# A fused attention and softplus FFN kernel: single load steps in the bias stage, four relus moved to ScalarE, four score tiles moved into round 0, and one round order for rounds 1 to 13

## The chip, the cores and the metric

The kernel runs on one core of a Trainium2 chip. The metric is the device time of one execution in microseconds (us). Five engines work beside each other, each through its own list of instructions in order: TensorE (PE; its weight loads are PEld), VectorE (DVE), ScalarE (ACT), GpSimd (POOL) and SyncE (SP), which here only issues DMA transfers. ScalarE issues some transfers too.

## What is computed

```python
scores = scale * np.matmul(q, k.transpose(0, 1, 3, 2))       # 4 batches, 8 heads, 576 x 576, head size 64
x = (psi_rel / psi_i)[..., None]                             # from the distance |i - j| and the row i
bias = np.maximum(x @ w1 + b1, 0.0) @ w2                     # a small MLP, 32 hidden units, one bias per head
attn = softmax(scores + bias.transpose(2, 0, 1))             # along the row, with 1e-9 in the divisor
h = (attn @ v, laid out as 2304 x 512) @ w_in                # FFN, 512 -> 2048 -> 512
out = (np.maximum(h, 0.0) + np.log1p(np.exp(-np.abs(h)))) @ w_out
```

The bias depends on head and position alone, so it is made once and kept in DRAM.

## The kernel before, in words

**Bias stage** (L868 to L888). 36 steps `s`, each for 16 rows of the bias. `emit_hid` makes four hidden tiles `m` of a step (relu of `lw` times a row's constant): three on VectorE, the fourth on ScalarE if `s` is in `RELU_ACT`, else on VectorE too. It runs `LEAD` = 5 steps ahead; 23 `m` tiles exist. `emit_mm` multiplies them on TensorE into `acc` (two of them), `emit_rows` copies `acc` on ScalarE in two pieces into a tile `e` (a ring of five, pool `wk`) and SP stores it to `e_d` in DRAM. Bias tiles `b` of 128 rows are loaded back from `e_d` by `emit_bias(pr, t)`, `t` from 0 to 8 (tiles 0 to 3 head one, 5 to 8 head two, tile 4 the last 64 rows of both). Tile 4 needs the last store.

**Rounds.** A round `n` (0 to 15) handles one pair of heads of one batch. Its nine score tiles `t` are made one round ahead: S is the product on TensorE into one of four PSUM places, A on VectorE adds the bias, takes the row's extreme and so empties the place (`first`), X is the exponential on ScalarE (`second`). T turns a block (TensorE), V copies it out of PSUM (suffix a on ScalarE, d on VectorE), P0 to P4 are the products with `vn`. I inverts the row sums, R turns them, C copies them and stores them to `r_d` (ScalarE's queue), G loads them back spread over 64 rows as `rb`, O multiplies the output by `rb` on VectorE, Y stores it. Z, ZA, ZX, ZL are S, A, X, L for the round itself, used in round 0. D is a dummy transpose. v, k, q, w, b issue loads; B are steps on the FFN's weights, whose tokens bring them in beside attention.

Within the bias stage some score tiles are made already: `STAGE` lists them by step, D for a whole tile of round 0 and R for a tile of round 1 that ScalarE copies out of PSUM unchanged (`raw`, L356), so that the bias can be added later.

**What sets the order.** The order of instructions on an engine is the order in which the program issues them: `ROUND0`, `ROUND1`, `ROUND` (rounds 2 to 13), `ROUND14` and so on are lists of tokens, a suffix such as `/2` naming the PSUM place. In rounds 0 and 1 the loads hang on token positions (`LOADS0`, `LOADS`), and O's and C's followers are deferred by a number of tokens (`defer`, `RB_AFTER` = 24). In the bias stage loads follow `LOAD_AT` and `early`. A DMA waits in its issuer's list until what it needs is there, and what stands behind it waits too. SP's list shows a few loads ahead of their place in the code, where nothing held them.

After round 16 comes the FFN on TensorE alone, unchanged here.

## Time and profile before

| | us |
|---|---|
| three runs | 673.45, 675.04, 809.87 |
| median of them | 675.04 |
| the profiled execution | 675.52 |
| its span, first to last instruction | 673.7 |
| TensorE busy | 643.7 (96%) |
| ScalarE busy | 513.0 (76%) |
| VectorE busy | 499.2 (74%) |

The profile is of one execution; times in it count from the span's start. "Busy" leaves out waiting. A row of waits or of the chain names the releaser: the work whose end let the engine go on. L numbers are lines of the kernel before.

### The profile page before, as it was taken

Reading aid. Unit: us, or ns where it says so; the run is one execution under the profiler, and the core shown is the slowest. Engines: PE = TensorE matmul, PEld = TensorE weight load, DVE = VectorE, ACT = ScalarE, POOL = GpSimd, SP = SyncE. Lnnn points to the kernel's source line nnn. Section 1 sums busy time; section 2 is a strip of 40 time slices with the busy share of each in tenths; the row PEclk is TensorE's granted clock in tenths of the full one; section 3 lists DMA queues with packets and bytes.
Section 4 is the critical chain, followed back from the end, with each engine's and each line's share of the span. In section 5 each row is a group of like instructions: output and inputs, shape, how many; then the busy total and the mean of one; then the engine's idle time right before and its main releaser. Section 6 shows DMA issues by size and latency. Waiting matters only on the chain.

```text
span 673.7 us, 13202 instructions
## 1 busy us (share of the span) xinstructions
PE 643.7 (96%) x4807; PEld 479.0 (71%) x4807; DVE 499.2 (74%) x1084; ACT 513.0 (76%) x1059; POOL 32.8 (5%) x103
## 2 busy tenths in 40 slices
PE   5689789999999998999999999999999999999997
PEld 2124446766767665778888888888888888888886
DVE  6976659999998998787786965796774556556564
ACT  6798769999999998897785867785775665665654
POOL 0000101111111110000000000000000000000000
PEclk9879789999999999999999999999999999999999
DMA  5876938868879646551321204230200322202220
GB/s 150 310 239 226 344 118 277 280 226 291 282 242 283 212 150 209 163 191 44 142 78 48 102 9 151 74 121 33 78 17 0 113 76 106 82 0 87 70 95 32
DMA packets 51040, 96.84 MB, mean 144 GB/s; under 512 B 7440, under 2 KB 19104, under 8 KB 50976
## 3 DMA queue, kind: packets, MB, share of 16 engines
q1 hardware_dynamic: 50208, 95.34, 42.1%
q8 instruction: 38, 0.62, 0.4%
q10 hardware_dynamic: 768, 0.66, 0.3%
q14 instruction: 26, 0.21, 0.1%
...
## 4 chain that ended last, share of the span: by engine, by line
PE 88%; DMA 5%; ACT 3%; DVE 1%; SPq 1%; issue 1%; ACTq 0%; DVEq 0%
PE y L842 29%; PE h L784 29%; PE o L470 11%; PE s L347 6%; PE s L411 4%; PE acc L236 3%; PE t L347 3%; DMA e_d<-e 2%; PE t L411 1%; ACT e L257 1%; PE o L347 1%; PE o L411 1%; DMA dist<-in_c_dist_dram 1%; DMA a<-w_d 1%; DMA b<-e_d 1%
## 5 line engine op out<-in xcount | busy, mean ns | idle before, releaser
L784 PE MATMUL h<-x,wi 128*128 128x512 f32 (+1 forms) x960 | 211.7, 370 | 0.1
L842 PE MATMUL y<-wo,g 128*128 128x512 f32 x864 | 209.8, 391 | 0.0
L784 PEld LDWEIGHTS h<-x,wi 128*128 128x128 f32 x960 | 169.5, 189 | 33.2 <-DVE wi L757 0.5
L842 PEld LDWEIGHTS y<-wo,g 128*128 128x128 f32 x864 | 161.3, 188 | 33.6 <-DVE g L816 0.2
L807 DVE SCALAR_TENSOR_TENSOR u<-u,e 128x512 f32<-128x512 f32 (+1 forms) x80 | 51.0, 638 | 103.4 <-ACT l L804 103.1
L383 ACT ACTIVATE p<-p,m 128x576 f32<-128x576 f32 x144 | 110.4, 768 | 5.9 <-DVE m L365 2.4
L800 ACT ACTIVATE e<-h 128x512 f32<-128x512 f32 (+1 forms) x80 | 44.2, 553 | 77.3 <-PE h L784 77.2
L470 PE MATMUL o<-pt,vn 128*64 128x256 f32 (+3 forms) x640 | 83.5, 424 | 0.0
L365 DVE CUSTOM_DVE_ANT_0 p<-s,b 128x576 f32<-128x576 f32 x79 | 58.5, 753 | 10.0 <-ACT e L257 3.3
L814 ACT ACTIVATE g<-l 128x512 fp32r<-128x512 f32 (+1 forms) x80 | 46.8, 585 | 19.3 <-DVE l L811 9.8
L347 PE MATMUL s<-kn,qn 64*128 64x288 f32 (+1 forms) x416 | 59.2, 419 | 0.2 <-ACT p L358 0.2
L470 PEld LDWEIGHTS o<-pt,vn 128*64 128x64 f32 (+1 forms) x640 | 37.6, 138 | 27.8 <-issue 8.7
L816 DVE TENSOR_TENSOR g<-l,g 128x512 fp32r<-128x512 f32 (+1 forms) x80 | 50.4, 629 | 3.7 <-ACT g L814 3.7
L236 PE MATMUL acc<-m,coef 128*32 128x512 f32 (+17 forms) x352 | 38.3, 537 | 15.0 <-ACT e L257 7.7
L316 ACT ACTIVATE pt<-s 128x384 f32<-128x384 f32 (+1 forms) x94 | 44.7, 483 | 8.1 <-ACT r L524 4.6
L811 DVE TENSOR_TENSOR l<-l,u 128x512 f32<-128x512 f32 (+1 forms) x80 | 50.6, 632 | 0.0
L809 DVE SCALAR_TENSOR_TENSOR l<-h,l 128x512 f32<-128x512 f32 (+1 forms) x80 | 50.5, 631 | 0.0
L804 ACT ACTIVATE l<-u 128x512 f32<-128x512 f32 (+1 forms) x80 | 47.2, 589 | 2.9
L801 ACT ACTIVATE e<-e 128x512 f32<-128x512 f32 (+1 forms) x80 | 47.2, 590 | 2.5
L803 ACT ACTIVATE u<-e 128x512 f32<-128x512 f32 (+1 forms) x80 | 47.2, 590 | 2.6
L223 DVE TENSOR_SCALAR m<-lw,pb 128x576 f32<-128x576 f32 (+17 forms) x122 | 44.3, 443 | 1.0 <-PE acc L236 1.0
L411 PEld LDWEIGHTS s<-ident,p 64*128 64x128 f32 x672 | 32.4, 141 | 17.3 <-DVE m L365 7.4
...
## 6 DMA issues: line engine op xcount, KB each, us to landing
e_d<-e SPq DMA_DIRECT2D x36, 295.5 KB, 3.4
...
```

What stands on the lines that cost most here:

```text
L236: nc.tensor.matmul(acc[32 * g:32 * g + 32, lo:hi], lhsT=coef.rearrange("p o h -> p (o h)"), rhs=hid[s, g][:, lo:hi], start=True, stop=True ...
L347: nc.tensor.matmul(ps[at:at + w, half, :SH], lhsT=q_n[n][rows, hd, c0:c0 + w], rhs=k_n[n][rows, hd], start=True, stop=True, tile_position= ...
L365: nc.vector.tensor_tensor_reduce(prob[n, t].rearrange("p (a c) -> p a c", a=2), st_["ps"], bias[pr, t].rearrange("p (a c) -> p a c", a=2), ...
L383: nc.scalar.activation(p, p, AF.Exp, bias=st_["m"], scale=-1.0, accum_out=ssum[n][:, PLACE.index(t):PLACE.index(t) + 1],)
L411: nc.tensor.transpose(ps[:, a, i], src[rows], ident[rows, 64 * a:64 * a + 64], tile_position=(64 * a, 0))
L470: nc.tensor.matmul(o[up, half, 0:w], lhsT=v_n[n][rows, jb, hd], rhs=pt[n, jb][rows, c0:c0 + w], start=(jb == 0), stop=(jb == 4), tile_posi ...
L784: nc.tensor.matmul(ps[:, :nb], lhsT=wi[f][:, a, 128 * c:128 * c + 128], rhs=xs[bi, c][:, x_, :nb], start=(i == 0), stop=(i == 11),)
L807: nc.vector.scalar_tensor_tensor(u, u, -1.0, e, op0=ALU.add, op1=ALU.subtract)
L809: nc.vector.scalar_tensor_tensor(l, ps, 0.0, l, op0=ALU.max, op1=ALU.add)
L811: nc.vector.tensor_tensor(l, l, u, op=ALU.subtract)
L816: nc.vector.tensor_tensor(g[:, 1], l, g[:, 0], op=ALU.subtract)
L842: nc.tensor.matmul(y, lhsT=g[:, a, 128 * ts:128 * ts + 128], rhs=wo[f][:, w_], start=(first and i == 0), stop=(last and i == 2),)
```

## The change

Line numbers in rows of the changed kernel are smaller, by 12 in the stage and by up to 48 at the end.

- Constants: `dist`, `tab`, then `wts`; the first batch's k and q no longer stand ahead of the stage.
- `RELU_ACT` gains steps 3, 6, 9 and 12.
- k and q of batches 0 and 1 are loaded singly after steps 0, 2, 5, 8; bias tiles 0, 5, 1, 6, 2, 7, 3, 8 singly after steps 11 to 35, where they came in pairs. k of batch 2 comes ahead of bias tile 4, q behind `vn`.
- Raw tiles of round 1: R11, R13, R18 and R14 go; tiles 1, 3, 8 and 4 are made in round 0 (S1, S3, S8, S4).
- `ROUND0` is rewritten with its loads as tokens and without D; round 1 uses `ROUND`. `defer`, `LOADS`, `LOADS0`, `ROUND1`, `STEADY` go. All `rb` loads are issued by SP.

```diff
-LOADS = {22: "b", 4: "q", 0: "v", 34: "w", 6: "k", 25: "b", 23: "b", 10: "b", 31: "b"}
-LOADS0 = {17: "k", 28: "v1", 71: "w", 6: "q", 59: "v"}
-RELU_ACT = {s for s in range(30) if s % 3 or not s} | {32}
-
-LOAD_AT = (2,)
-LATE = 3
+RELU_ACT = {s for s in range(30) if s % 3 or s < 13} | {32}
+
+LOAD_AT = {0: (0, "k"), 2: (0, "q"), 5: (1, "k"), 8: (1, "q")}
+EARLY = ((11, 0), (14, 5), (18, 1), (22, 6), (26, 2), (29, 7), (34, 3), (35, 8))
 STAGE = """
-21:D00 21:R15 24:R16 25:R10 26:R12 26:D01 27:D05 29:R17 31:R11 31:R13 32:D02 33:D06 33:R18
-34:R14
+21:D00 21:R15 24:R16 25:R10 26:R12 26:D01 27:D05 29:R17 31:D02 33:D06
 """
...
-    nc.sync.dma_start(out=wts, in_=mlp)
     nc.sync.dma_start(out=dist, in_=c_dist.to_broadcast([128, S]))
     nc.sync.dma_start(out=tab[:, 0:212], in_=c_tab)
+    nc.sync.dma_start(out=wts, in_=mlp)
...
-                queue(n).dma_start(
+                nc.sync.dma_start(
                     out=t[64 * hd:64 * hd + 64, lo:hi],
...
-    emit_load(0)
     nc.sync.dma_start(out=ident, in_=c_id)
...
-    early = {8 * t + 7: (t, t + 5) for t in range(3)}
+    early = {s: (t,) for s, t in EARLY}
...
         if s in LOAD_AT:
-            emit_load(1 + LOAD_AT.index(s))
-        for t in early.pop(s - LATE, ()):
+            emit_load(*LOAD_AT[s])
+        for t in early.pop(s, ()):
             emit_bias(0, t)
...
-    for t in (3, 8, 4):
-        emit_bias(0, t)
+    emit_load(2, "k")
+    emit_bias(0, 4)
     emit_load_v(0)
-    emit_load(2)
+    emit_load(2, "q")
...
         if n < 3:
-            tiles = [(1, t) for t in ((), range(5), range(5, 9))[n]]
+            tiles = [(1, t) for t in ((0,), (1, 2, 4, 3), (8, 7, 5, 6))[n]]
...
-        toks = {0: ROUND0, 1: ROUND1, N - 2: ROUND14, N - 1: ROUND15, N: ROUND16}.get(n, ROUND).split()
+        toks = {0: ROUND0, N - 2: ROUND14, N - 1: ROUND15, N: ROUND16}.get(n, ROUND).split()
...
-            if tok == "C" and n not in STEADY:
-                defer(RB_AFTER, lambda n=n: units["r", n][2]())
```

`ROUND0` after the change:

```
v1 Z7/0 T10/o S1/1 ZA7 V10/a Z3/2 T20/0 ZX7 A1 V20/a k q T00/o S3/1 ZA3 X1 V00/d Z8/0 T30/2 ZX3 A3
V30/a ZL1 ZL2 A2 S8/1 ZA8 X3 T40/2 V40/a A0 ZX8 Z4/0 A8 ZL3 T12/o V12/d X2 T22/2 V22/a S4/1 w ZA4
T02/o V02/d X0 L0 T32/2 V32/a A4 ZX4 ZL4 I T01/2 V01/d R/0 T11/o C G v V11/a T21/2 V21/d A7 X8 P0 X4
L4 A5 P1 T31/0 V31/a T41/2 V41/d X7 A6 P2 X5 b L1 L2 X6 L3
```

What moves on the engines, at three places.

SP in the bias stage, before; `e_d<-e` is a step's store, kn and qn are k and q of a batch, `b<-e_d` a bias tile:

```order
L869 DMA ident<-in_c_id_dram 128x128
L261 DMA e_d<-e 128x591 x3
L279 DMA kn<-in_k_dram 128x2x288
L285 DMA qn<-in_q_dram 128x1152
L261 DMA e_d<-e 128x591 x8
L306 DMA b<-e_d 128x576
L308 DMA b<-e_d 128x576
L261 DMA e_d<-e 128x591 x8
L306 DMA b<-e_d 128x576
L308 DMA b<-e_d 128x576
L261 DMA e_d<-e 128x591 x8
```

The same place after:

```order
L837 DMA ident<-in_c_id_dram 128x128
L249 DMA e_d<-e 128x591
L267 DMA kn<-in_k_dram 128x2x288
L249 DMA e_d<-e 128x591 x2
L273 DMA qn<-in_q_dram 128x1152
L249 DMA e_d<-e 128x591 x3
L267 DMA kn<-in_k_dram 128x2x288
L249 DMA e_d<-e 128x591 x3
L273 DMA qn<-in_q_dram 128x1152
L249 DMA e_d<-e 128x591 x3
L294 DMA b<-e_d 128x576
L249 DMA e_d<-e 128x591 x3
```

The pair k and q behind the third store, and the pairs of bias tiles, are taken apart; k and q of the first batch join them among the stores.

ScalarE at the end of the bias stage, before; `e<-acc` are a step's two copies, `p<-s` a raw copy, `p,ss<-p,m` an exponential, `pt<-` a V copy:

```order
L358 ACTIVATE p<-s_82 128x576
L257 ACTIVATE e<-acc,tab 128x64
L257 ACTIVATE e<-acc,tab 128x527
L358 ACTIVATE p<-s_83 128x576
L257 ACTIVATE e<-acc,tab 128x48
L257 ACTIVATE e<-acc,tab 128x543
L257 ACTIVATE e<-acc,tab 128x32
L257 ACTIVATE e<-acc,tab 128x559
L358 ACTIVATE p<-s_82 128x576
L257 ACTIVATE e<-acc,tab 128x16
L257 ACTIVATE e<-acc,tab 128x575
L383 ACTIVATE p,ss_117<-p,m 128x576
```

The same place after:

```order
L371 ACTIVATE p,ss_117<-p,m 128x576
L245 ACTIVATE e<-acc,tab 128x64
L245 ACTIVATE e<-acc,tab 128x527
L245 ACTIVATE e<-acc,tab 128x48
L245 ACTIVATE e<-acc,tab 128x543
L245 ACTIVATE e<-acc,tab 128x32
L245 ACTIVATE e<-acc,tab 128x559
L245 ACTIVATE e<-acc,tab 128x16
L245 ACTIVATE e<-acc,tab 128x575
L371 ACTIVATE p,ss_117<-p,m 128x576 x2
L304 ACTIVATE pt<-o 128x2x3x64
L371 ACTIVATE p,ss_117<-p,m 128x576
```

The raw copies between the steps' copies are gone (R11, R13 and R18 here), and behind the last copy ScalarE goes to two exponentials and the first V copy of round 0.

ScalarE in rounds 0 and 1, before, around the row sums of round 0; `r<-t` is C's copy, `r_d<-r` its store, `rb<-r_d` the loads of G, `p,ss<-p,m` exponentials, `pt<-` V copies:

```order
L524 ACTIVATE r<-t 9x128
L525 DMA r_d<-r 9x128
L383 ACTIVATE p,ss_118<-p,m 128x576
L383 ACTIVATE p_1099,ss_119<-p_1099,m 128x576
L316 ACTIVATE pt<-s_82 128x2x3x64 x2
L531 DMA rb<-r_d 64x576
L531 DMA rb<-r_d 64x320
L531 DMA rb<-r_d 64x256
L524 ACTIVATE r<-s_83 9x128
L525 DMA r_d<-r 9x128
```

SP from the loads behind bias tile 4 on, after:

```order
L280 DMA vn<-in_v_dram 128x640
L273 DMA qn<-in_q_dram 128x1152
L280 DMA vn<-in_v_dram 128x640
L267 DMA kn<-in_k_dram 128x2x288
L273 DMA qn<-in_q_dram 128x1152
L667 DMA r<-in_moe_w_in_dram 128x512
L516 DMA rb<-r_d 64x576
L516 DMA rb<-r_d 64x320
L516 DMA rb<-r_d 64x256
L280 DMA vn<-in_v_dram 128x640
L294 DMA b<-e_d 128x576
```

The three loads of `rb` left ScalarE's list, where an exponential of round 0, one of round 1's and two copies stood ahead of them, and stand on SP, ahead of a load of `vn` and a bias tile; ScalarE keeps the copy and the store.

## Rows read from the trace of the kernel before

**Rows 1.** The page's head: span and number of instructions.

```profile
span 673.7 us, 13202 instructions
```

**Rows 2.** Chain of waits: start us, length us, engine, tile, line, count.

```profile
118.14 0.54 PE o L347 x4
...
130.48 0.54 PE o L347 x4
```

**Rows 3.** Busy us by stretch (count of instructions), granted clock, DMA share, GB/s.

```profile
62.80:80.60 17.80, 12.66 (x135) 7.65 (x131) 10.99 (x31) 14.55 (x38) 2.57 (x9) 0.81 0.83 304
80.60:99.30 18.70, 15.44 (x166) 8.54 (x164) 10.86 (x28) 10.57 (x26) 1.80 (x5) 0.91 0.55 181
```

In rows 3 and 8 the columns are length, then busy time of PE, PEld, DVE, ACT and POOL.

**Rows 4.** The same, sum over 10.2 to 62.8 us.

```profile
sum 52.60, PE 44.52 PEld 13.07 DVE 45.82 ACT 46.11 POOL 0.00; mean PE 11.13 PEld 3.27 DVE 11.46 ACT 11.53 POOL 0.00
```

**Rows 5.** Timeline of ScalarE, bias stage: start, length, work, [idle before <- releaser].

```profile
10.20 0.90 ACT L257 ACTIVATE e<-acc,tab 128x576 f32<-128x576 f32 x2 [0.91 <-PE acc L236]
11.00 0.71 ACT L221 ACTIVATE m<-lw,pb 128x496 f32<-128x496 f32 x1
11.60 1.72 ACT L257 ACTIVATE e<-acc,tab 128x560 f32<-128x560 f32 x4
...
21.43 0.90 ACT L257 ACTIVATE e<-acc,tab 128x448 f32<-128x448 f32 x2 [1.91 <-DMA e_d<-e]
...
33.70 0.90 ACT L257 ACTIVATE e<-acc,tab 128x304 f32<-128x304 f32 x2 [1.06 <-DMA e_d<-e]
```

**Rows 6.** Chain of waits from the start to round 1.

```profile
1.17 4.58 DMA dist<-in_c_dist_dram
...
14.80 6.53 DMA e_d<-e
...
62.80 3.81 DMA e_d<-e
...
67.30 4.25 DMA b<-e_d
...
75.23 2.12 PE o L470 x8
...
79.56 1.12 PE o L470 x8
...
85.85 3.74 DMA rb<-r_d
```

**Rows 7.** Timeline of SP's queue, bias stage.

```profile
14.21 0.49 SPq L285 DMA_DIRECT2D qn<-in_q_dram  x1
```

**Rows 8.** Busy us in stretches of two us, as in rows 3.

```profile
20.00:22.00 2.00, 0.57 (x8) 0.00 (x0) 2.00 (x7) 0.56 (x2) 0.00 (x0) 1.00 1.04 398
...
24.00:26.00 2.00, 2.00 (x16) 0.26 (x8) 2.00 (x8) 1.46 (x5) 0.00 (x0) 0.50 0.55 213
```

**Rows 9.** Timeline of TensorE around the end of the bias stage.

```profile
64.12 0.40 PE L411 MATMUL s<-ident,p 64*128 64x64 f32 x6 [1.04 <-ACT p L358]
...
71.87 0.58 PE L411 MATMUL t<-ident,p 64*128 64x64 f32 x6 [3.12 <-ACT p L383]
```

**Rows 10.** Timeline of VectorE, round 1: the multiplication by rb.

```profile
89.72 0.82 DVE L490 TENSOR_TENSOR x<-o,rb 128x256 f32<-128x256 f32 x2 [4.15 <-DMA rb<-r_d]
```

**Rows 11.** Groups by line, 0 to 66 us: count, busy us, mean ns, idle before.

```profile
L223 DVE TENSOR_SCALAR m<-lw,pb 128x576 f32<-128x576 f32 (+17 forms) x122 | 44.3, 443 | 1.0 <-PE acc L236 1.0
...
L221 ACT ACTIVATE m<-lw,pb 128x464 f32<-128x464 f32 (+17 forms) x22 | 14.2, 658 | 4.6 <-DVE pb L200 4.6
...
L358 ACT ACTIVATE p<-s 128x576 f32<-128x576 f32 x9 | 5.9, 666 | 0.6 <-PE s L347 0.6
```

**Rows 12.** The page's DMA issues: count, KB each, median us to landing.

```profile
e_d<-e SPq DMA_DIRECT2D x36, 295.5 KB, 3.4
```

**Rows 13.** Timeline of ScalarE's queue, rounds 0 and 1.

```profile
79.89 0.55 ACTq L525 DMA_DIRECT2D r_d<-r  x1
...
84.67 1.79 ACTq L531 DMA_DIRECT2D rb<-r_d  x3
```

More of the change, by code (lines that the diff above doesn't have):

```diff
@@ L50 @@
 """
-STEADY = range(2, 17)
 SETS = ((2, 4), (3, 8), (7, 5, 6), (1, 0))
 ROUND0 = """
-A6 A2 Z7 T10/1 A7 Z3 T20/0 V20/a T30/o A0 T00/2 ZA7 V00/d V30/a V10/a A1 A5 D6 Z8 X7 X2 ZX7 ZA3 X5
-X6 ZA8 A3 ZX3 ZX8 Z4 ZA4 ZL1 ZL3 ZX4 A8 D14 T22/2 T40/1 T32/o ZL4 V32/d T02/0 V22/a V02/a T01/o X0
-T11/2 V40/d T21/1 V11/a ZL2 V01/d V21/d L2 T12/0 P0 X8 L0 X1 I V12/d T41/1 A4 P1 X4 T31/0 R/2
-V41/a C P2 V31/d L3 X3 L4 L1
-"""
-ROUND1 = """
-I S4 T20/0 S3 A4 T11/1 A3 T00/2 S2 P3 X4 V00/d V20/a T02/0 V11/d T12/2 V02/a R/1 C P4 T41/0 S7
-T22/1 S0 A2 O V12/a T01/o V41/a T10/0 V22/d L4 B0 T21/2 V01/a X3 A7 S1 V10/d P0 V21/a A0 T31/0
-X2 T32/2 S5 X7 A1 P1 S6 V31/a V32/d X0 S8 B1 T30/1 X1 B2 L0 A5 T40/0 V30/a B3 L1 A8 V40/a X8 A6
-X6 L3 P2 B4 X5 L2
+v1 Z7/0 T10/o S1/1 ZA7 V10/a Z3/2 T20/0 ZX7 A1 V20/a k q T00/o S3/1 ZA3 X1 V00/d Z8/0 T30/2 ZX3 A3
+V30/a ZL1 ZL2 A2 S8/1 ZA8 X3 T40/2 V40/a A0 ZX8 Z4/0 A8 ZL3 T12/o V12/d X2 T22/2 V22/a S4/1 w ZA4
+T02/o V02/d X0 L0 T32/2 V32/a A4 ZX4 ZL4 I T01/2 V01/d R/0 T11/o C G v V11/a T21/2 V21/d A7 X8 P0 X4
+L4 A5 P1 T31/0 V31/a T41/2 V41/d X7 A6 P2 X5 b L1 L2 X6 L3
 """
@@ L509, in inv @@
         nc.vector.reciprocal(s_, s_)
-    def queue(n):
-        return nc.scalar if n < 2 else nc.sync
     def u_r(n):
@@ L593, in emit @@
         elif kind in ("Z", "ZA", "ZX"):
-            stage(("s", n, *a), u_s, ("Z", "ZA", "ZX").index(kind))
+            stage(("s", n, *a), u_s, ("Z", "ZA", "ZX").index(kind), *on)
         elif kind == "L":
@@ L610, in emit @@
                 stage(("x", n - 1), u_x, 0)
-                if n not in STEADY:
-                    defer(8, lambda: stage(("x", n - 1), u_x, 1))
         elif kind == "B":
@@ L616, in emit @@
                 stage(("b", i), u_bits, *a)
-                if a[0] == 4 and n not in STEADY:
-                    defer(8, lambda: stage(("b", n - 1), u_bits, 5))
         elif kind in ("k", "q"):
-            emit_load(n + 3, kind)
+            emit_load(n + (a[0] if a else 3), kind)
         elif kind == "v":
-            emit_load_v(n + 2)
+            emit_load_v(n + (a[0] if a else 2))
         elif kind == "w":
@@ L650, in emit @@
             assert False, tok
-    waiting = []
-    def defer(k, f):
-        waiting.append([k, f])
-    def passed():
-        for w in list(waiting):
-            w[0] -= 1
-            if w[0] < 0:
-                waiting.remove(w)
-                w[1]()
     def bits(pl, src, eng, pb_=None):
@@ L975, in tile_log_bias_attention__then__softplus_ffn @@
             s_use[0] = 0
-        toks = {0: ROUND0, 1: ROUND1, N - 2: ROUND14, N - 1: ROUND15, N: ROUND16}.get(n, ROUND).split()
-        for i, tok in enumerate(toks):
-            load = {0: LOADS0, 1: LOADS}.get(n, LOADS if n > N - 2 else {}).get(i)
-            if load in ("k", "q"):
-                emit_load(n + 3, load)
-            elif load == "v":
-                emit_load_v(n + 2)
-            elif load == "v1":
-                emit_load_v(n + 1)
-            elif load == "w":
-                pre_load(n)
-            elif load == "b" and tiles:
-                emit_bias(*tiles.pop(0))
-            emit(n, tok)
-            if tok == "C" and n not in STEADY:
-                defer(RB_AFTER, lambda n=n: units["r", n][2]())
-            passed()
-    while waiting:
-        passed()
+        toks = {0: ROUND0, N - 2: ROUND14, N - 1: ROUND15, N: ROUND16}.get(n, ROUND).split()
+        for tok in toks:
+            emit(n, tok)
     es_m.close()
```

1 line of the change is left out of this document (removed).

## The prediction

> **What bounds the kernel now.** The profiled execution took 675.5 us, of which the span is 673.7 [rows 1]; the median of the three runs is 675.0, so the sum below is made on 675.5 and reads the same on the median. A difference under 2% (13.5 us) is about what a measurement of this kernel cannot tell from no change.
>
> I read the chain of waits first, then busy time by stage. From about 106 us on, the chain is TensorE work only: round 3 and round 4 repeat the same score tile 12.34 us apart [rows 2]. The change leaves everything from round 2 on in its old order, so only the time before round 2, which starts at 99.3 us, can move. That time has three stretches: the bias stage to 62.8, round 0 of 17.8 and round 1 of 18.7 us [rows 3]. A round costs 12.34 when TensorE is full, so round 1 alone carries 6.4 us of waste.
>
> In the bias stage the engine with least room is ScalarE: from the first bias row's copy to the last it works 46.11 of 52.60 us [rows 4]. VectorE runs ahead of it. Of the 6.5 us idle, 1.91 and 1.06 are waits for a store `e_d<-e` to land [rows 5]: the five `e` tiles are a ring, and step 8 needs step 3's store, which the chain shows taking 6.53 us [rows 6]; step 17 needs step 12's. The first was issued at 14.80, right behind the pair k and q of batch 1 (288 and 576 KB; q's issue is at 14.21 [rows 7]), the second in the wake of the first two bias loads. TensorE was busy 0.57 us of 20 to 22, and in 24 to 26 its granted clock is 0.50 (1.2 instead of 2.4 GHz) [rows 8]; after a gap of 3.12 us before 71.87 [rows 9] a P block (a product with v) takes 2.12 us at 75.23 where one at 79.56 takes 1.12 [rows 6]; after one of 1.04 us before 64.12 nothing of the kind shows.
>
> Behind the stage the chain goes: last store 3.81 us, bias tile 4's load 4.25, then the slow P block, then the load `rb<-r_d`, for which VectorE sits idle 4.15 us [rows 6, 10].
>
> **The change, part by part.**
>
> *Constants' order.* `dist` is issued first instead of second. Its issue stood at 1.17 [rows 6], so it may start 0.43 earlier; k and q no longer follow it at once. `wts`, also needed, now goes third. Bounds: 0.4 us lost (if `wts` lands last) to 1.2 gained. I take 0.6, since the large k and q stop sharing the engines with it: first copy at 9.6 instead of 10.2.
>
> *Four relus to ScalarE.* A relu of 496 columns occupies it from 11.00 to 11.60 [rows 5], so steps 3, 6, 9, 12 (528, 480, 432, 384 columns) cost 0.63, 0.59, 0.54, 0.50. Step 3's fits in the 0.91 us in which ScalarE waits for the first accumulator [rows 5]; the others add 1.6 us to the engine that bounds. VectorE saves four at 0.44 [rows 11] and gains nothing, for it was ahead. This part alone is a loss.
> The Trainium skill, "ScalarE: Activation LUTs", section "Rules for kernel authors", says to put relu on VectorE, not ScalarE, and budgets about 0.3 us plus 0.83 ns an element; an estimate by that page is 0.7, 0.66 and 0.62, so 2.0 us, and the sum would be 0.4 longer than with the row's occupancy. The trace agrees in direction: 658 ns on ScalarE against 443 on VectorE.
>
> *Four raw copies fewer.* R11, R13 and R18 stood before the last copy, R14 behind it. One takes 0.67 [rows 11], about 0.1 of it overlapped as for the relu: 1.6 us off ScalarE before the end. This cancels the relus, so ScalarE's floor stays 46.1.
>
> *Loads in small steps.* k and q of batches 0 and 1 now stand singly after steps 0, 2, 5, 8; one k and seven bias tiles come singly later. The ring allows a store five steps of about 1.2 us, less copy and issue: some 4.7, against a median landing of 3.4 [rows 12]. At 400 GB/s, about what the engines reach in 20 to 22 [rows 8], a 288 KB load adds 0.7 and q's 576 KB adds 1.4: inside for the former, at the edge for the latter. So I let both waits go (3.0 us). With them goes what caused the half-clock stretch in rows 8, in which ScalarE waits for accumulators too, so I take 1.1 of the remaining 3.5 us of small pieces. Idle 2.4: last copy ends at 9.6 + 46.1 + 2.4 = 58.1, against 62.8, so 4.7 us gained. Bounds: idle 0 (55.7) and unchanged 6.5 (62.2).
>
> *Round 0.* The four score tiles go to TensorE in round 0 (4 x 0.54 [rows 2], beside 12.66 busy of 17.8 [rows 3], much of that at half clock), and VectorE reads them straight from PSUM. ScalarE has the same 13 exponentials either way, one transposed copy more and R14 less, so it keeps its 14.5 us [rows 3], hidden under the rest as long as it is fed. What sets the end is bias tile 4: store 3.81 plus load 4.25 and two issues, 8.9 us after the last copy as now. Bias tiles 3 and 8 are issued later (after steps 34 and 35); they are wanted ahead of tile 4, and the work before them (two or three tiles on VectorE) covers them. From tile 4's landing (71.55) to round 1's first score tile (80.6) it takes 9.1 now, with the same work behind the tile in the new order: subtraction, exponential, reciprocal, transposes, three P blocks. At full clock the first P block is 1.0 shorter, and the transposes and the second block around it I put at 0.8: 7.3 us. TensorE runs out of other work about 2 us before tile 4's transpose (eight score tiles and nine transposes are some 6 to 7 us, ahead of a point some 10 us after the last copy, with ScalarE's pace spread between), between the gap that kept the clock and the one that lost it [rows 9]; the dummy transposes are gone too. So 16.2 to 18.0; I take 16.9. Round 1 starts at 58.1 + 16.9 = 75.0, against 80.6.
>
> *Round 1* takes the steady order. `rb` now is issued by SP right behind its store instead of 24 tokens later on ScalarE's queue: today the row sum's store goes at 79.89 and the load not before 84.67 [rows 13]. About 9 us (its 4.5 KB store 2.5, an estimate under the 295 KB stores' 3.4, three issues 1.8 [rows 13], load 3.74 [rows 6], handovers) after its transpose it is there; in the new order x wants it about 9 us after that transpose. So the 4.15 us wait shrinks to at most one. SP's queue waits there for the store; behind it stand v, a bias tile and weights, wanted a round later. ScalarE enters with two exponentials (1.5 us) still to do, where the steady round has 0.6 us to spare. Bounds 12.34 and 16; I take 13.3, against 18.7.
>
> **Sum.** Round 2 starts at 88.3 against 99.3: 11.0 us gained (4.7 + 0.9 + 5.4). 675.5 - 11.0 = 664.5.
>
> **Rivals.**
> *The gain stays in round 1 only.* ScalarE's idle pieces move instead of going, and the clock falls in round 0 as now: 62.2 + 18.0 + 13.3 = 93.5, so 669.7. For it: ScalarE's work is not smaller, and TensorE waits for ScalarE there. Against: two waits have a cause that is taken away.
> *The clock stays up.* No gap of TensorE reaches 2 us: idle 0.9 (56.6), round 0 15.6, round 1 12.5: 84.7, so 660.9, which is faster by 2.1%. For it: the half-clock stretches follow the waits that go. Against: bias tile 4 still comes late.
> *Slower: each load among the stores stalls ScalarE as the pair k and q did.* Twelve loads stand between the stores; at 1.91 each they cost 22.9, less the 3.0 paid now, so +19.9, while rounds 0 and 1 give back 6.3: 689. It decides from 0.8 us a load on, where nothing is gained at all. Against: most loads are a third of that pair, and a store has about 1.3 us to spare.
>
> **Chances.** Forecast 664.5, own range 661.5 to 668: 0.60. Only round 1: 0.15. Clock up: 0.21. Slower: 0.04, of which I count 0.03 past 2%. That makes faster 0.21, same 0.76, slower 0.03. The bounds of the unknown costs end at 659 (every lower one, less what would have to coincide) and 672; the range 659 to 671 leaves out under 2 in 10.
>
> **What would show it.** ScalarE's idle before `e<-acc` with releaser `DMA e_d<-e` gone; last copy near 58; SP's loads with no store above 4.7 us to landing. P blocks at 1.12 in round 0 speak for the clock rival, at 2.12 against. `x` (L490's counterpart) without a wait for `rb`. Score tile to score tile from round 1 to round 2 near 13.3. Wrong if a wait for a store is back behind q, if VectorE waits for bias tiles 3 or 8, or if round 1 is above 16.

## The result, and the profile after

The changed kernel takes 665.22 us (median of four runs, 664.71 to 665.65), the kernel before 674.27 beside it: a ratio of 0.987, 95% interval 0.985 to 0.989. One of the four runs of the kernel before, 809.87 us, was in a slow state and is not in the ratio. That is 1.3% faster: less than the 2% that the prediction took for the limit of what a measurement can tell, but clear of no change. The forecast was 664.5, and the span is 662.9 where 662.7 was expected. The sum came out almost right; of its terms two did not.

The head of the page after, and the same three stretches on which [rows 3, 4] stand for the kernel before. Columns: stretch, its length, busy us (and instructions) of PE, PEld, DVE, ACT and POOL, granted clock, DMA share, GB/s.

```profile
span 662.9 us, 13180 instructions
```

```profile
9.34:59.26 49.92, 40.53 (x379) 11.07 (x371) 42.97 (x121) 45.38 (x105) 0.00 (x0) 0.97 0.87 291
```

```profile
59.26:76.73 17.47, 13.68 (x144) 7.85 (x145) 12.01 (x33) 13.26 (x37) 2.42 (x8) 0.90 0.72 236
76.73:89.30 12.57, 12.57 (x167) 8.74 (x166) 10.35 (x30) 11.93 (x31) 2.09 (x6) 1.00 0.84 275
```

The first stretch is the bias stage from first copy to last, then round 0 and round 1, each counted to the first TensorE instruction of the next round's list. Against the forecast:

| | before | forecast | after |
|---|---|---|---|
| first bias row's copy starts | 10.20 | 9.6 | 9.34 |
| last bias row's copy ends | 62.77 | 58.1 | 59.26 |
| round 0, length | 17.83 | 16.9 | 17.47 |
| round 1, length | 18.70 | 13.3 | 12.57 |
| round 2 starts | 99.31 | 88.3 | 89.30 |
| span | 673.7 | 662.7 | 662.9 |

Round 2 starts 10.0 us earlier, not 11.0. The span gained 10.8, because in the kernel before round 2 still had something to make up: its score tile in place `o` follows its start after 6.3 us before (105.63 less 99.31) and after 5.8 now (95.09 less 89.30). From there on both kernels repeat the same period, as [rows 2] showed.

TensorE, the score tile into place `o`, rounds 1 to 3 of the changed kernel (start, length, tile):

```profile
82.75 0.70 PE L335 MATMUL o<-kn,qn 64*128 64x288 f32 x4
95.09 0.70 PE L335 MATMUL o<-kn,qn 64*128 64x288 f32 x4
107.44 0.70 PE L335 MATMUL o<-kn,qn 64*128 64x288 f32 x4
```

12.34 and 12.35 apart: the full-TensorE period is reached one round earlier than before. The first of these rows, counted from the last bias copy, is the mark by which the experiments below are compared: 82.75 less 59.26 is 23.49 us for round 0 and the piece of round 1 up to it.

**One wait for a store stayed.** ScalarE in the bias stage after, its three telling rows (in brackets the idle time before the row and its releaser), which answer to [rows 5]:

```profile
9.34 0.90 ACT L245 ACTIVATE e<-acc,tab 128x576 f32<-128x576 f32 x2 [0.33 <-PE acc L224]
13.44 0.93 ACT L245 ACTIVATE e<-acc,tab 128x528 f32<-128x528 f32 x2
29.05 0.90 ACT L245 ACTIVATE e<-acc,tab 128x352 f32<-128x352 f32 x2 [2.08 <-DMA e_d<-e]
```

SP's queue ahead of that wait (issue start, length), and the piece of the chain of waits that it belongs to:

```profile
21.39 0.42 SPq L273 DMA_DIRECT2D qn<-in_q_dram  x1
22.30 2.39 SPq L249 DMA_DIRECT2D e_d<-e  x3
```

```profile
22.30 6.64 DMA e_d<-e
```

The store behind q of batch 1 (step 9's) takes 6.64 us to land, as the one behind the pair k and q took 6.53 before [rows 6]. Step 14 wants its `e` tile at 26.97, and ScalarE stands 2.08 us. TensorE stands with it, and its granted clock falls:

```profile
30.01 4.38 PE L224 MATMUL acc<-m,coef 128*32 128x320 f32 x32 [2.21 <-ACT e L245]
```

```profile
12.00:30.00 18.00, 11.77 (x112) 2.15 (x104) 17.33 (x53) 15.88 (x38) 0.00 (x0) 1.00 0.99 325
30.00:34.00 4.00, 3.95 (x32) 0.71 (x32) 2.61 (x8) 3.77 (x10) 0.00 (x0) 0.57 0.84 292
```

The first of these two rows bears on the wait as much as the queue does: over 18 us the DMA engines are busy 0.99 of the time and move 325 GB/s. The same stretch of the kernel before:

```profile
12.00:30.00 18.00, 13.86 (x131) 2.87 (x124) 18.00 (x55) 15.56 (x38) 0.00 (x0) 0.91 0.88 282
```

The share was 0.88 there. The change brought k and q of the first batch into this stretch, which stood ahead of the stage before. And 282 over 0.88 is 320 GB/s: over a stretch with stores and loads the engines reach 320 to 325 GB/s in the mean, not the 398 of [rows 8] on which the prediction's price of a load was made. That row is no price of a load at all. Its packets, in the kernel before from 20 to 22 us:

```profile
DMA packets 377, 0.80 MB, mean 398 GB/s; under 512 B 43, under 2 KB 43, under 8 KB 376
```

In the trace's packet records all 333 packets of 2 to 8 KB are 2,364 bytes long, a row of a store (591 numbers of 4 bytes); none is a row of k (1,152 bytes) or q (4,608). So 398 GB/s is the rate of stores alone. In the changed kernel the rate at a full share goes up and down with what moves. Two rows, the first behind the issue of q of batch 0 (at 13.40 us), the second behind that of a bias tile (24.81):

```profile
14.00:16.00 2.00, 1.39 (x16) 0.32 (x16) 2.00 (x6) 2.00 (x6) 0.00 (x0) 1.00 1.03 241
26.00:28.00 2.00, 1.37 (x16) 0.16 (x8) 2.00 (x8) 0.97 (x3) 0.00 (x0) 1.00 1.02 377
```

Added up by size from 12 to 30 us, the packets of the two q loads took 4.3 us of the 16 engines' time and those of the two k loads 2.2, so 2.2 us for a q and 1.1 for a k. The stores' median landing rose from 3.4 us [rows 12] to 4.0:

```profile
e_d<-e SPq DMA_DIRECT2D x36, 295.5 KB, 4.0
```

The Trainium skill, "DMA: Bandwidth & Descriptors", section "Specifications", gives some 358 GB/s as the HBM limit of one core. The trace does not bear it out as a limit over two us (398 in [rows 8], 377 above); the 18 us row stays under it with 325. For a load's price in a mixed stretch the measured 325 decides, which is below both 358 and 398.

**Round 0 is ScalarE's.** From 59.16 to 69.05 it works without a gap (ten exponentials and six V copies); then the row sums' copy, their store, and the next V copy. The chain of waits runs over ScalarE there:

```profile
62.29 1.51 ACT p L371 x4
...
68.30 0.76 ACT p L371 x2
```

Bias tile 4 is not what holds it: the second half's load is issued at 62.88, and VectorE adds the tile (second row) without a wait.

```profile
62.88 0.59 SPq L299 DMA_DIRECT2D b<-e_d  x1
66.94 0.75 DVE L353 CUSTOM_DVE_ANT_0 p<-s,b 128x576 f32<-128x576 f32 x1
```

ScalarE's rows behind the gapless stretch, then TensorE's P blocks from the chain of waits, then the clock:

```profile
70.05 0.27 ACT L509 ACTIVATE r<-s 9x128 f32<-9x128 f32 x1 [1.00 <-PE s L399]
70.35 0.56 ACTq L510 DMA_DIRECT2D r_d<-r  x1
71.01 0.49 ACT L304 ACTIVATE pt<-o 128x384 f32<-128x384 f32 x1 [0.69 <-DMA r_d<-r]
```

```profile
71.56 3.60 PE o L458 x16
...
75.68 1.12 PE o L458 x8
```

```profile
72.00:74.00 2.00, 2.00 (x12) 0.99 (x10) 0.50 (x2) 1.01 (x4) 0.53 (x2) 0.50 0.44 174
```

The first two P blocks take 3.60 us together with the clock at 0.50 (1.2 GHz) for most of them; two blocks at 1.12, as the third in the second row, would be 2.24.

**Round 1 lost its wait for `rb`.** SP issues the three loads at 73.71, and the multiplication waits 0.26 us for TensorE alone, where it waited 4.15 for `rb` [rows 10]:

```profile
73.71 1.73 SPq L516 DMA_DIRECT2D rb<-r_d  x3
```

```profile
81.11 0.82 DVE L478 TENSOR_TENSOR x<-o,rb 128x256 f32<-128x256 f32 x2 [0.26 <-PE o L458]
```

### The profile page after: what moved, and what is told of

It is laid out like the page before. It is cut to its first block, busy times and chain, and to the rows that moved or that the text cites. A ratio compares the mean times of both kernels' runs of the same rounds, so it can differ in the third digit from the quotient of the medians.

```text
span 662.9 us, 13180 instructions
## 1 busy us (share of the span) xinstructions
PE 637.7 (96%) x4800; PEld 477.0 (72%) x4800; DVE 497.2 (75%) x1079; ACT 512.2 (77%) x1060; POOL 33.1 (5%) x103
## 4 chain that ended last, share of the span: by engine, by line
PE 91%; ACT 5%; DMA 2%; DVE 1%; issue 1%; SPq 0%; ACTq 0%; DVEq 0%
PE y L811 29%; PE h L753 29%; PE o L458 12%; PE s L335 6%; PE s L399 4%; PE acc L224 4%; PE t L335 3%; ACT e L245 2%; PE t L399 1%; PE o L335 1%; ACT p L371 1%; DMA e_d<-e 1%; PE o L399 1%; DMA wts<-in_mlp_dram 0%; ACT pt L304 0%
## 5 line engine op out<-in xcount | busy, mean ns | idle before, releaser
L458 PE MATMUL o<-pt,vn 128*64 128x256 f32 (+3 forms) x640 | 82.0, 421 | 1.2 <-ACT pt L304 1.0
L353 DVE CUSTOM_DVE_ANT_0 p<-s,b 128x576 f32<-128x576 f32 x82 | 60.7, 753 | 6.7 <-PE s L335 3.4
L224 PE MATMUL acc<-m,coef 128*32 128x512 f32 (+17 forms) x352 | 36.6, 511 | 15.1 <-ACT e L245 8.8
L211 DVE TENSOR_SCALAR m<-lw,pb 128x576 f32<-128x576 f32 (+17 forms) x118 | 42.9, 441 | 2.1 <-PE acc L224 2.1
L335 PEld LDWEIGHTS s<-kn,qn 64*128 64x128 f32 (+1 forms) x412 | 31.6, 170 | 12.3 <-DVE m L353 1.8
## 6 DMA issues: line engine op xcount, KB each, us to landing
e_d<-e SPq DMA_DIRECT2D x36, 295.5 KB, 4.0
```

The source lines that it names most:

```text
L224: nc.tensor.matmul(acc[32 * g:32 * g + 32, lo:hi], lhsT=coef.rearrange("p o h -> p (o h)"), rhs=hid[s, g][:, lo:hi], start=True, stop=True ...
L335: nc.tensor.matmul(ps[at:at + w, half, :SH], lhsT=q_n[n][rows, hd, c0:c0 + w], rhs=k_n[n][rows, hd], start=True, stop=True, tile_position= ...
L353: nc.vector.tensor_tensor_reduce(prob[n, t].rearrange("p (a c) -> p a c", a=2), st_["ps"], bias[pr, t].rearrange("p (a c) -> p a c", a=2), ...
L458: nc.tensor.matmul(o[up, half, 0:w], lhsT=v_n[n][rows, jb, hd], rhs=pt[n, jb][rows, c0:c0 + w], start=(jb == 0), stop=(jb == 4), tile_posi ...
```

## The experiments

Eleven kernels ran: eight are the changed kernel with one part undone or altered, one is the kernel before with one part of the change alone, and two combine alterations. Each line below gives the median and the ratio to the kernel before with its 95% interval, and from the profile two marks: the end of the last bias copy, and the time from there to the score tile in place `o` of round 1 (59.26 and 23.49 in the changed kernel). The marks are of one execution each, and they vary without any edit: two of the kernels below have the changed kernel's stage untouched and end it at 58.90 and 60.65, and the kernel before with `rb` by SP, whose stage is untouched too, ends it 1.89 us later than the kernel before. So a difference of a mark below some 2 us shows little by itself. The ratios are each to runs of the kernel before made beside that kernel.

| | us | ratio (interval) | last copy ends | from there to the mark |
|---|---|---|---|---|
| changed kernel | 665.22 | 0.987 (0.985 to 0.989) | 59.26 | 23.49 |
| relus as before | 665.69 | 0.986 (0.983 to 0.989) | 60.60 | 23.56 |
| first batch's k and q ahead | 666.94 | 0.988 (0.984 to 0.992) | 61.15 | 25.49 |
| loads of the stage as before | 668.01 | 0.989 (0.986 to 0.993) | 61.31 | 24.91 |
| round 1 in the old order | 667.55 | 0.989 (0.985 to 0.993) | 58.90 | in round 2, see there |
| kernel before, `rb` by SP | 674.76 | 1.002 (1.000 to 1.004) | 64.66 | in round 2, see there |
| `rb` of round 0 late | 667.32 | 0.990 (0.988 to 0.992) | 60.65 | 25.27 |
| raw copies as before | 668.88 | 0.993 (0.991 to 0.995) | 62.24 | 25.59 |
| ring of seven | 663.01 | 0.985 (0.982 to 0.988) | 56.50 | 25.79 |
| q of batch 1 six steps later | 669.34 | 0.992 (0.990 to 0.994) | 63.13 | 24.48 |
| ring of seven, bias tiles 3, 8 a step earlier | 662.73 | 0.983 (0.980 to 0.985) | 56.98 | 23.80 |
| the same, dummies, V copy first | 661.80 | 0.981 (0.979 to 0.984) | 56.41 | 23.67 |

### The relus back to VectorE

```diff
-RELU_ACT = {s for s in range(30) if s % 3 or s < 13} | {32}
+RELU_ACT = {s for s in range(30) if s % 3 or not s} | {32}
```

> The changed kernel with the relus of steps 3, 6, 9, 12 back on VectorE; all else as changed (665.2 us, last copy of the bias stage ends at 59.3). Theory A (the stage's early part is held by how fast the DMA engines carry the stores and the four k and q loads, their busy share is 0.96 to 1.03 from 12 to 28 us): ScalarE gets to the ring of e tiles earlier and waits there longer, last copy within 0.6 of 59.3, 664.6 to 665.8 in all. Theory C (ScalarE's own work is the floor, as the prediction's sum had it): 1.6 us less work on ScalarE shows in full, last copy near 57.7, 663.6. Theory V (VectorE needed the relief): last copy later than 60.

665.69 us, the changed kernel's time within the interval. By the prediction's sum ScalarE had 1.6 us less to do; it used none of it. Its copies, grouped over 0 to 62 us, here and in the changed kernel (count, busy us, mean ns, then the idle time before them and what ended it):

```profile
L245 ACT ACTIVATE e<-acc,tab 128x576 f32<-128x576 f32 (+35 forms) x72 | 32.4, 514 | 7.8 <-DMA e_d<-e 3.8 <-ACT e L245 2.2 <-PE acc L224 1.5
```

```profile
L245 ACT ACTIVATE e<-acc,tab 128x576 f32<-128x576 f32 (+35 forms) x72 | 33.2, 540 | 4.9 <-ACT e L245 2.4 <-DMA e_d<-e 2.1 <-PE acc L224 0.3
```

The waits for stores rose from 2.1 to 3.8 us, and those for the accumulator from 0.3 to 1.5. So in this stretch the ring and its stores set the pace, not ScalarE's work: what is taken off ScalarE comes back as waiting. The last copy, at 60.60, lies outside theory A's 0.6 us and in theory V's range; but an untouched stage ended at 60.65, so the mark decides nothing on VectorE. The theory that ScalarE's sum of work sets the stage's end (663.6) falls. The prediction said "This part alone is a loss"; within the intervals it is none.

### The first batch's loads ahead of the stage

```diff
-LOAD_AT = {0: (0, "k"), 2: (0, "q"), 5: (1, "k"), 8: (1, "q")}
+LOAD_AT = {5: (1, "k"), 8: (1, "q")}
...
     nc.sync.dma_start(out=ident, in_=c_id)
+    emit_load(0)
```

> The changed kernel, but k and q of batch 0 are issued right behind the constants again (after dist, tab, wts, ident), so that 864 KB leave the stretch of 10 to 28 us; k and q of batch 1 stay after steps 5 and 8. Theory A (too many bytes in the stretch): ScalarE's wait of 2.08 us for a store behind q of batch 1 goes; the start may be 0 to 0.9 us later; last copy at 57.2 to 58.5, 663.2 to 664.5 in all. Theory B (one 576 KB load ahead of a store is enough by itself): a wait of 1.5 us or more stays behind q, last copy at 59.3 or later, 665 or more.

666.94 us, no gain. (Two of the four runs took 665.2 and 665.3 us, two 668.6 and 668.7; the trace is of one of the longer two.) The stretch of 12 to 16 us has room now (DMA share 0.50), yet the wait is there at the same step:

```profile
17.79 0.43 SPq L267 DMA_DIRECT2D kn<-in_k_dram  x1
18.74 2.03 SPq L249 DMA_DIRECT2D e_d<-e  x2
20.83 0.43 SPq L267 DMA_DIRECT2D kn<-in_k_dram  x1
21.35 0.44 SPq L249 DMA_DIRECT2D e_d<-e  x1
21.85 0.42 SPq L273 DMA_DIRECT2D qn<-in_q_dram  x1
```

```profile
29.16 0.90 ACT L245 ACTIVATE e<-acc,tab 128x352 f32<-128x352 f32 x2 [2.00 <-DMA e_d<-e]
```

The run does not separate the causes cleanly, for the second of these loads, k of batch 2, moved here of itself (presumably because its tile was free earlier), so that 1,152 KB are issued within 4.1 us, where it is 864 KB within 3.9 us in the changed kernel. What it shows is that a wait at 27 us needs neither a full queue at 14 nor a share near 1 over the whole 18 us: the share of 12 to 30 us is 0.82 here, and near 1 only from 20 us on. A second wait for a store, 1.52 us, stands at step 24.

### The loads of the stage as they were

```diff
-LOAD_AT = {0: (0, "k"), 2: (0, "q"), 5: (1, "k"), 8: (1, "q")}
+LOAD_AT = {2: (1,)}
...
-    early = {s: (t,) for s, t in EARLY}
+    early = {8 * t + 10: (t, t + 5) for t in range(3)}
```

(with k and q of batch 0 ahead of `ident`, and bias tiles 3 and 8 and k and q of batch 2 behind the stage, as before)

> The changed kernel with the loads of the bias stage as before the change (k and q of batch 0 ahead, of batch 1 as a pair behind the third store, bias tiles in pairs after steps 10, 18, 26 and the rest at the end); constants, relus, raw tiles and rounds stay changed. By the prediction (single steps take 3.0 us of waits away): last copy at 62 to 63, 668 to 669. By theory A (the waits only moved, 2.97 before and 2.08 now): last copy 59.8 to 61, 665.7 to 667. If the old loads cost nothing: 59.3 and 665.2.

668.01 us. ScalarE's two waits:

```profile
21.20 0.91 ACT L245 ACTIVATE e<-acc,tab 128x448 f32<-128x448 f32 x2 [0.72 <-DMA e_d<-e]
...
42.80 0.91 ACT L245 ACTIVATE e<-acc,tab 128x192 f32<-128x192 f32 x2 [1.96 <-DMA e_d<-e]
```

The second belongs to a store issued at 35.74 behind a pair of bias tiles, 6.95 us to landing. The stage ends 2.05 us later: 0.6 by these waits (2.68 against 2.08), 0.26 by the later start, the rest in small pieces. The mark comes 1.4 us later still, 0.4 of it in the first two P blocks (4.01 us). By the medians the small steps are worth some 2.8 us, though the intervals overlap and the stage's 2.05 us are hardly more than an untouched stage varies by. It is not shown that they work in the way that was meant: the waits are nearly as long with them as without.

### Round 1 in its old order

(the old list of round 1 with its loads as tokens; `rb` of round 0 stays with SP, `rb` of round 1 is taken 24 tokens later as before)

> The changed kernel with round 1 in its old order (its loads at the old places, G 24 tokens after C, as tokens; rb issued by SP); round 0 stays changed, so rb of round 0 still is loaded right behind its store. Round 1 takes 12.57 us changed, 18.70 before. If both the order and the early rb of round 0 count: 15 to 16.5 us, 668 to 669 in all. If rb alone made the gain: under 14, below 666.5. If the order alone made it: over 17.5, above 670.

667.55 us. The score tile in place `o` of round 2 starts at 96.70, which is 37.80 us behind the last copy. In the changed kernel it is 35.83 (95.09 less 59.26), in the kernel before 42.86 (105.63 less 62.77). So of the 7.0 us that lie behind the stage, the order of round 1 has 2.0, and what else changed behind the stage (round 0's new list and the early `rb`) 5.1. The ratio's interval overlaps the changed kernel's.

### The kernel before, with `rb` by SP right behind the row sums

```diff
-RB_AFTER = 24
+RB_AFTER = 0
...
-        return nc.scalar if n < 2 else nc.sync
+        return nc.sync
```

> The kernel before, with one part of the change alone: the loads of rb in rounds 0 and 1 are issued by SP right behind C instead of by ScalarE 24 tokens later. Before takes 674.5 us; VectorE waits 4.15 us for rb in round 1 and TensorE is at half clock behind it. If that wait is the larger part of what round 1 lost: 670 to 671.5, and round 1 takes 14.5 to 15.5 us instead of 18.7. If the order of round 1 holds it up at the same place for another reason: 673.5 or more.

674.76 us, no gain (ratio 1.000 to 1.004), although the wait named in [rows 10] is gone. The trace is of the longest of ten runs, 678.12 us; its stage ended 1.89 us later than in the kernel before. Three views: VectorE's multiplication, SP's queue, and ScalarE:

```profile
89.17 0.82 DVE L490 TENSOR_TENSOR x<-o,rb 128x256 f32<-128x256 f32 x2 [1.10 <-PE s L347]
```

```profile
91.96 1.73 SPq L531 DMA_DIRECT2D rb<-r_d  x3
...
98.93 0.58 SPq L698 DMA_DIRECT2D r<-in_moe_w_out_dram  x1
```

```profile
103.33 0.66 ACT L673 ACTIVATE a<-r 128x512 f32<-128x512 f32 x1 [3.76 <-DMA r<-in_moe_w_out_dram]
```

SP's list now waits for round 1's row sums until 91.96, and for four stores of `x` behind it; the FFN weights behind those are issued at 98.93 (at 92.37 in the kernel before; against the last copy, 4.7 us later), and ScalarE, whose next instruction wants them, stands 3.76 us. TensorE has a gap of 3.13 us at 105.04, and the granted clock is 0.50 in 106 to 108. Round 2's score tile in place `o` starts at 108.45, 43.79 us behind the last copy (42.86 in the kernel before). The wait for `rb` was exchanged for another of about the same length. In the changed kernel the list of loads is another: the same weights are issued at 76.59, behind `rb`, one load of `vn` and one bias tile.

### `rb` of round 0 late again, in the new order

```diff
-R/0 T11/o C G v V11/a ... X5 b L1 L2 X6 L3
+R/0 T11/o C v V11/a ... X5 b L1 L2 X6 G L3
```

(on ScalarE's queue in round 0)

> The changed kernel, with the loads of rb of round 0 put back on ScalarE's queue, 24 tokens behind C (at the end of round 0). Changed 665.2 us. If the early issue is needed in the new order too: x waits for rb by 2 to 4 us and TensorE's clock falls behind the gap, 667 to 669.5. If the new order of round 1 leaves x enough time: under 666.

667.32 us, and the wait is back:

```profile
84.43 0.82 DVE L478 TENSOR_TENSOR x<-o,rb 128x256 f32<-128x256 f32 x2 [2.05 <-DMA rb<-r_d]
```

The mark comes 1.8 us later (25.27 against 23.49). The medians differ by 2.1 us, though the intervals overlap by a little. So the early `rb` is worth some 1.8 to 2 us here; in the kernel before, whose lists are others, it was worth nothing. The gap of TensorE behind the wait is 0.99 us, and the granted clock stays at 1.00 there, so the fall of the clock that was expected did not come.

### The raw copies back in the stage

```diff
-29:R17 31:D02 33:D06
+29:R17 31:R11 31:R13 32:D02 33:D06 33:R18
+34:R14
```

(S1, S3, S8 and S4 leave round 0)

> The changed kernel with score tiles 1, 3, 8 and 4 of round 1 made in the bias stage again and copied raw by ScalarE (R11, R13, R18, R14), and not in round 0. Changed: last copy ends at 59.3, 665.2 us. Theory C (ScalarE's work is the floor): last copy 1.6 later, 60.9, and what round 0 saves is under 0.5: 666.3 to 667. Theory A (the stores hold the stage, so three copies fall into waits): last copy 59.3 to 60, 665 to 666. If round 0 is relieved by four tiles on TensorE: 664.5 or less.

668.88 us, the largest loss by a part undone, and the only part undone whose interval (0.991 to 0.995) lies clear of the changed kernel's. The last copy ends 3.0 us later, of which the three raw copies ahead of it are 2.0; waits for stores of 1.22 and 1.63 us stand where one of 2.08 stood. The mark comes 2.1 us later still, with the first two P blocks at 4.11 us instead of 3.60:

```profile
75.56 4.11 PE L459 MATMUL o<-pt,vn 128*64 128x256 f32 x16 [0.82 <-ACT pt L305]
```

The prediction had 1.6 us for this part.

### A ring of seven

```diff
-mk = pool(es_b, "mk", 23)
+mk = pool(es_b, "mk", 21)
...
-wk = pool(es_b, "wk", 5)
+wk = pool(es_b, "wk", 7)
```

> The changed kernel with seven e tiles in the ring instead of five (and 21 hidden tiles m instead of 23, to make room). It takes away what makes ScalarE wait, the ring, not the DMA traffic. If the one wait of 2.08 us behind q of batch 1 is a latency: it goes, the half-clock stretch at 30 to 34 us goes, last copy 56.5 to 57.5, 662.3 to 663.5 in all. If the DMA engines are short of rate over the whole stage: ScalarE waits later instead, last copy 58.5 or later, 664.5 or more.

663.01 us. The stores land no sooner, even later in the median, but ScalarE waits for none:

```profile
e_d<-e SPq DMA_DIRECT2D x36, 295.5 KB, 5.4
```

From 12 to 30 us ScalarE is busy 18.00 of 18.00 us, at a DMA share of 0.98. The last copy ends 2.76 us earlier, at 56.50: the wait of 2.08 and its wake were the ring's. But the mark gains 0.46 only. The stores land later, and bias tile 3, which needs them, with them: its load is issued 0.25 us ahead of the last copy's end, where it was 1.24 us (at 58.02) in the changed kernel. VectorE in round 0, TensorE's first P blocks, and the clock:

```profile
59.65 0.76 DVE L353 CUSTOM_DVE_ANT_0 p<-t,b 128x576 f32<-128x576 f32 x1 [0.71 <-DMA b<-e_d]
```

```profile
70.53 4.08 PE L458 MATMUL o<-pt,vn 128*64 128x256 f32 x16 [0.83 <-ACT pt L304]
```

```profile
64.00:74.00 10.00, 8.05 (x68) 4.57 (x68) 5.69 (x16) 5.38 (x14) 1.34 (x5) 0.51 0.69 239
```

The granted clock is at half for ten us, and 2.3 of the 2.76 us are given back up to the mark. The first expectation's numbers came, and the second's later wait did not: from first copy to last the DMA share is 0.91, so the shortage is of the dense piece, and two more tiles carry ScalarE over it.

### q of batch 1 six steps later

```diff
-LOAD_AT = {0: (0, "k"), 2: (0, "q"), 5: (1, "k"), 8: (1, "q")}
+LOAD_AT = {0: (0, "k"), 2: (0, "q"), 5: (1, "k"), 14: (1, "q")}
```

> The changed kernel with q of batch 1 (576 KB) moved from behind step 8 to behind step 14. In SP's list k of batch 2 (288 KB) then takes the place that q had, between the stores of steps 8 and 9; q stands between the stores of steps 14 and 15, beside bias tile 5. Theory A (the size of the load right ahead of a store delays that store, and the store's ring delays ScalarE): the wait of 2.08 us at step 14 falls under 0.7, and one of 1.5 to 2.5 us comes back six steps later, at step 20, behind q; last copy within 1 us of 59.3, time 664 to 667. Theory B (it is the sum of bytes queued by then, not the one load): with 288 KB fewer queued the wait at step 14 falls to about 1, and nothing new shows at step 20; last copy 58.0 to 58.5, time 663 to 664.5. Theory C (the size plays no part, the wait comes from the stores alone): the wait of about 2 at step 14 stays.

669.34 us, and none of the three theories holds whole. ScalarE's waits:

```profile
28.42 0.90 ACT L245 ACTIVATE e<-acc,tab 128x352 f32<-128x352 f32 x2 [1.69 <-DMA e_d<-e]
...
38.40 0.90 ACT L245 ACTIVATE e<-acc,tab 128x256 f32<-128x256 f32 x2 [2.86 <-DMA e_d<-e]
```

The interval (0.990 to 0.994) lies just clear of the changed kernel's. Theory A is right in kind on step 20, where a wait of 2.86 us, longer than it said, stands behind q and bias tile 5; it is wrong on step 14, where k's 288 KB in place of q's 576 leave 1.69 of 2.08. So q is not needed for the wait at step 14, and yet a wait follows it to step 20; the last copy, at 63.13, is 3.9 us later than in the changed kernel, where theory A allowed 1. The DMA share of 12 to 30 us is 0.98 at 316 GB/s. What fits this run and the two that moved loads before, though no run shows it by itself, is a queue near full in the piece ahead of the wait. Worked out for the changed kernel from 12 to 30 us (a KB of the view is 1,024 bytes): a store of 295.5 KB every 1.3 us, the distance of the copies at 20 us, is 233 GB/s; two k, two q and a bias tile, 2,016 KB in 18 us, are 115; together 348, and the engines move 325. By this reading each load pushes the stores behind it, until a wait of ScalarE lets the queue drain.

### The larger ring with the last bias tiles a step earlier

```diff
-EARLY = ((11, 0), (14, 5), (18, 1), (22, 6), (26, 2), (29, 7), (34, 3), (35, 8))
+EARLY = ((11, 0), (14, 5), (18, 1), (22, 6), (26, 2), (29, 7), (33, 3), (34, 8))
```

(with the ring of seven)

> The changed kernel with a ring of seven e tiles (and 21 in place of 23 hidden tiles), as before, and bias tiles 3 and 8 loaded one step earlier, behind steps 33 and 34. If the late bias tiles 3 and 8 are what took back the gain of the larger ring in round 0: VectorE's wait for bias tile 3 (the one before the additions at about 60 us) goes, the granted clock stays at 1.00 to 70 us, both first P blocks take under 3.7 us together, and the first score tile of round 2 starts 24 us after the last copy (25.8 with the ring alone, 23.5 in the changed kernel): 661 to 662.5. If SP, which now waits for the store of step 31 ahead of the last three stores, hands the wait on to bias tile 4: its load is issued later than 4 us behind the last copy, and the time is 663 or more.

662.73 us. VectorE's wait for bias tile 3 is gone, the granted clock is 1.00 up to 68 us, and the mark comes 23.80 us behind the last copy instead of 25.79: in the traces the late bias tile was what took back the ring's gain. The medians differ by only 0.28 us, well within the intervals. Bias tile 4 pays a little: its load is issued 4.55 us behind the last copy (3.04 in the changed kernel), and VectorE waits 0.30 us for it. The first two P blocks still take

```profile
69.26 3.85 PE L458 MATMUL o<-pt,vn 128*64 128x256 f32 x16 [1.00 <-ACT pt L304]
```

which is over the 3.7 that was expected.

### The same with dummies, and the V copy ahead of the row sums

```diff
-X0 L0 T32/2 V32/a
+X0 L0 T32/2 D4 V32/a
...
-T01/2 V01/d R/0 T11/o C G v V11/a
+T01/2 D3 V01/d R/0 T11/o V11/a C G v
```

> As the run before, and in round 0 seven dummy transposes on TensorE, where it otherwise stands idle ahead of the row sums' transpose, and the V copy of block 11 ahead of the row sums' copy and store on ScalarE. If the clock is what makes the first two P blocks slow: they take 2.3 to 3.0 us together in place of 3.6 to 4.1, the granted clock of their stretch is 1.00, and the time is 1.0 to 1.8 us under the run before. If the P blocks are slow for want of their operands (the V copy of block 11 comes late): the copy's earlier place alone gives some 0.7, with the clock at 0.50 as before. If neither: no difference, or up to 0.7 longer, since rb is stored later.

661.80 us, ratio 0.979 to 0.984: the fastest of all, and clear of the changed kernel's 0.985 to 0.989; against the run before it the intervals overlap. TensorE and the clock in this place:

```profile
66.56 0.66 PE L619 MATMUL o<-ident 128*128 128x128 f32 x4 [1.66 <-DVE pt L306]
...
69.24 3.15 PE L458 MATMUL o<-pt,vn 128*64 128x256 f32 x16 [0.27 <-ACT pt L304]
```

```profile
68.00:70.00 2.00, 1.73 (x19) 1.31 (x20) 1.12 (x3) 0.67 (x3) 0.00 (x0) 0.50 1.02 367
```

The wait for the V copy fell from 1.00 to 0.27 us, and the blocks from 3.85 to 3.15. But the row sums' transpose behind the dummies starts later against the last copy (11.56 us behind it, 10.46 in the run before), and the mark gains only 0.13 us; the rest of the 0.68 between the two profiled executions is a stage that ended 0.57 earlier with no edit in it. The medians differ by 0.93. Nor did the clock stay up: it is 0.50 already from 68 us on, and the mean from 68 to 74 us is 0.73, against 0.72 in the run before. The half-clock time came earlier, so that less of it fell on the P blocks. VectorE waited 1.11 us for a bias tile as well. So neither theory is shown: the pieces moved, and the sum hardly changed.

## Why the prediction was right, and where it was wrong

**The bound.** That only the time before round 2 can move held: the period of 12.34 us stands unchanged, and the span gained what the mark of round 2 gained (10.54) and 0.3 more.

**Constants' order.** Forecast 0.6, measured 0.86 (10.20 to 9.34). Right.

**Four relus.** That step 3's relu fits into the wait for the first accumulator is right: the wait is 0.33 after and 0.96 with the relus back. "The others add 1.6 us to the engine that bounds" is wrong as a cost, because ScalarE's work is not what bounds this stretch as long as the ring makes it wait: with the relus back it waits longer and the time is the same. With the ring of seven ScalarE is busy 18.00 of 18.00 us; what the relus cost there, no run shows.

**Four raw copies.** Forecast 1.6, measured some 3.7 by the medians (668.88 less 665.22). The term was counted as ScalarE's time alone; with the copies back the stage ended 3.0 us later and round 0 behind it ran 2.1 longer, in one execution. That the two cancel, and so ScalarE's work stays 46.1, was near (45.38), but it was not the work that mattered.

**Loads in small steps.** This is the step that failed: "So I let both waits go (3.0 us)". One stayed, 2.08 us behind q, and with it a half-clock stretch. ScalarE's idle time came out at 4.5 us (49.92 less 45.38), not 2.4, and the stage gained 3.5 us instead of 4.7. Two numbers under the step were wrong. The rate of a load was taken as 400 GB/s from two us in which only stores moved [rows 8]; so a k was priced at 0.7 us and a q at 1.4, and their packets took 1.1 and 2.2. And each load was priced alone against a store's slack, where the engines are busy 0.99 of 18 us; that their delays then add up is what the waits suggest. The row for it could have been read before: 12 to 30 us of the kernel before has share 0.88 at 282 GB/s, and the change moves 864 KB into it. Where the prediction named its own falsifier ("a wait for a store is back behind q") it was that one which came. The ring of seven shows the other side: without the waits the last copy ends at 56.50, next to the 56.6 of the rival in which the clock stays up.

**Round 0.** Forecast 16.9, measured 17.47. "What sets the end is bias tile 4" is wrong: its halves are issued at 62.30 and 62.88, and VectorE waits for no bias tile there. "ScalarE ... hidden under the rest" is wrong as well: it works from 59.16 to 69.05 without a gap, and the row sums follow its last exponential. What was right is that the first P blocks run at half clock for most of their time, which costs 1.4 us there (3.60 less 2.24). But the gap of about 2 us on which the prediction hung this did not come: from 66 us to the P blocks no gap of TensorE is longer than 1.01 us, about the one that kept the clock in [rows 9], and the clock fell all the same.

**Round 1.** Forecast 13.3 within 12.34 to 16, measured 12.57. The wait for `rb` is gone whole, and TensorE is busy for the whole of the round. The prediction left up to one us of waiting; there was none. The kernel before with `rb` by SP alone shows that this term was not `rb`'s alone: by itself it brings nothing, since SP's list then holds back weights. That another wait takes the place of the one removed was seen in the kernel before, not in the changed one.

**Sum.** Short by 1.2 in the stage and 0.5 in round 0 (0.4 gained, not 0.9), over by 0.7 in round 1: 1.0 less up to round 2; behind it 0.8 came that the sum did not have, since it ended at round 2's start. So 664.5 against 665.2 is right partly by errors of both signs.

**The rivals.** *The gain stays in round 1 only* (669.7): no, though its mechanism, waiting that moves instead of going, is what the relus' run shows. *The clock stays up* (660.9): no; it fell in 30 to 34 us and around 72 us. With the larger ring and the bias tiles earlier the stage's waits and one of these two stretches are gone, and the time is 661.8 to 662.7, so the figure was near for conditions that still were not all met. *Each load stalls ScalarE* (689): no; single bias tiles cost no wait in the changed kernel. But stores behind dense loads did land late: the run with q six steps later (669.34) has waits of 1.69 and 2.86 us.

What stays open: what exactly puts a wait on one store of a dense piece rather than on the next. The three runs that moved loads agree with a queue near full, but no run took the stores' bytes down to test it directly. No run put the constants back in their old order; their 0.86 us rest on the start of the first copy, 9.12 to 9.60 us in the eleven traces with the new order and 10.20 and 10.46 in the two with the old one. And what would keep the clock up in round 0 was not found: the dummies did not.
